# Attention scores as 64x64 tiles, keys and queries in one transfer, and another order of the first batch's transfers

## The chip, the core and the metric

The kernel runs on one core of a Trainium2 chip. The metric is the device time of one execution in microseconds (us), lower is better. TensorE (PE in the profile) multiplies; VectorE (DVE), ScalarE (ACT) and GpSimd (POOL) do the rest; SyncE (SP) computes nothing and issues transfers, as ACT and POOL also can. Each engine works through its own instructions in the order in which the program issued them.

## The reference, cut to what matters

```python
# q, k, v: 8 batches x 8 heads x 576 positions x 64, float32
scores = q @ k.T / 8
# heads 0-3: the last 32 positions; heads 4-7: every 4th of the last 128
attn = softmax(where(mask, scores, -1e9))
x = (attn @ v) -> (8, 576, 512)
u = x + real(fft(fft(x, axis=1), axis=2))
un = layernorm(u)
out = u + relu(un @ w_ch1) @ w_ch2        # 512 -> 2048 -> 512
```

## The kernel before

All work is written down as operations with an engine, a cost, a priority and the buffers that they read and write. `Plan.run` then plays a list scheduler: each engine takes, among the operations whose inputs are there, the one of lowest priority number, and the order found in this way is the program of that engine. So costs and priorities in the text change the order of instructions, not only what they say.

Attention. A pair is two heads of one batch, and each batch has four pairs (two of the plain window, two of the dilated one, whose positions the host has reordered so that its window also is a band). `attend_pair` requests the keys (two transfers of 64 partitions, into the two diagonal blocks of a tile `kb` whose other blocks stay zero), the queries (one transfer, tile `tq`) and the values (`vt`). It then calls `attend` twice (u = 0 and 1), which the text calls an attend: 64 of them in all, 8 in a batch. An attend has 8 or 10 blocks of 64 queries. For each block one float32 matmul contracts all 128 partitions (line 617: queries of both heads against keys of one head and zeros) into 64 partitions and 96 columns of one PSUM bank. Two banks (`sc`) take turns, so that one attend's scores can be written while the last one's are read. DVE adds the mask and takes the row maximum (L636), ACT takes the exponential (L642), PE transposes the probabilities (L656), ACT copies them out of PSUM (L658, L662), PE multiplies with the values (L669), and DVE normalises into `xt` and, for the last 64 positions, `xl` (L682, L687). The `xl` tag has one buffer, so the plain pairs' `xl` has to wait until the dilated pairs' has been stored.

Mix. `store` sends the result to DRAM scratch in the order that the transform wants (for the plain pairs of batch 0 straight into SBUF tiles). `fold` loads it back (L814, L823) and adds mirrored rows (L826, L828, L840, L842). `along_seq` (L877) and `along_channels` (L923) are the two Fourier transforms as matmuls. `normalise` makes the rows of the feed-forward input, `turned` (L771, L779) transposes them for batch 0.

Feed-forward. 6 of the 16 blocks of the hidden dimension are run in the first part, as a `fill` for each pair of token tiles: 72 matmuls up (L1053), 36 down (L1069). Their weights, float64 in DRAM, are prepared on the chip (L995 to L1015) through the same ring of four buffers (`ut`) that holds the feed-forward inputs; buffers of a ring are handed out strictly in the order of the text. The other ten blocks run at the end (L1334, L1432, L1399), when attention's memory is free.

PSUM banks are lent between tags. The first `NPT2` attends use a bank that later belongs to `mix`, and the first `NAV2` attends one that later belongs to `ff`:

```python
views["av2"] = [pt_av[1], zs[0]]
views["pt2"] = [pt_av[0], mixes[1]]
plan.behind.update({"av": ("av2",), "ff": ("av2",), "pt": ("pt2",), "mix": ("pt2",)})
```

`behind` means that the first buffer of a tag is handed out only when every buffer of the other tag is done. So the first `mix` matmul comes after 14 attends, and the first fill after 21.

Until `ff` is first used, PE runs filler matmuls on a tile of zeros (L542) when nothing else is ready; they have the lowest priority of all and no result.

Of the kernel before, what the change touches and what calls it, by code (L numbers as in the profile page):

```python
# [9 lines left out]
F32 = mybir.dt.float32  # L10
# [17 lines left out]
NKB = 2  # L28
NV = 3
NTQ = 2  # L30
# [10 lines left out]
NPT2, NAV2 = 14, 21  # L41
NGANG = 4
NU0, NU1 = 9, 9
NFD, NUD, NLW = 1, 0, 0
P_QK0, P_V0 = -8, -7
P_ST, P_FD, P_WD, P_ST0, P_FD0, P_SPAN0, P_SPAN1 = -9.92, -2.8, -14.79, -21.37, -25.12, 7.59, 23.92
P_QK, P_V, P_TR, P_MIX, P_SPAN, P_W, P_WF, P_FILL, P_FILLT = -7.53, -11.06, -5.0, 3.7, 13.0, 27.01, 3.96, 47.55, 3.61
P_MIX0, P_MIX1 = -24.21, 7.67
NSEQ, NCHN = 3, 7
# [5 lines left out]
WIN = 32  # L55
DIL = 4
# [107 lines left out]
def columns(x):  # L164

    return np.ascontiguousarray(by_pair(x).swapaxes(4, 5).reshape(B, 2, 2, P, S))
# [14 lines left out]
class Buf:  # L181


    def __init__(self, make=None, tag=None, ap=None):
        self.make, self.tag, self.ap = make, tag, ap
        self.writer, self.readers = {}, {}
        self.left = 0
        self.free_at = None
# [11 lines left out]
PSUM_TAGS = ("sc", "pt2", "av2", "pt", "av", "mix", "ff", "duo0", "duo1", "duo2")  # L200


class Plan:
# [21 lines left out]
    def add(self, eng, cost, fn, r=(), w=(), prio=0.0, nbytes=0, at=0.0):  # L225
# [15 lines left out]
        for items, writes in ((r, False), (w, True)):  # L241
            for it in items:
# [7 lines left out]
                else:  # L250
                    b.readers.setdefault(key, []).append(op.num)
        op.bufs = list(bufs.values())
# [8 lines left out]
    def run(self):  # L261
# [5 lines left out]
        dma = 0.0  # L267
# [36 lines left out]
        while events:  # L304
# [4 lines left out]
            while again:  # L309
                again = False  # L310
                for eng in busy:
# [48 lines left out]
                    if got.nbytes:  # L360
                        dma = max(dma, end + 0.9) + got.nbytes / (PIPE0 if end < T_PIPE else PIPE1)
                        done = dma + 1.6
                        lanes[eng].append(done)
                        heapq.heappush(events, done)
# [55 lines left out]
def fused_kernel(ctx: ExitStack, tc, q, k, v, w1, w2, seq, tail, chn, alt, mask, ident, perm, flip, out):  # L420
# [24 lines left out]
    views = {"sc": pair, "pt": pt_av[:1], "av": pt_av[1:], "mix": mixes, "ff": zs}  # L445
# [4 lines left out]
    plan.behind.update({"duo0": ("sc",), "duo1": ("pt", "av"), "duo2": ("mix",)})  # L450
# [27 lines left out]

    flip_sb = Buf(ap=const.tile([P, 16], I32, name="flip_sb")[:, 0:8])
# [25 lines left out]
    kbs = [fixed(heads, [P, 2, WIN + S], F32, f"kb{i}") for i in range(NKB)]  # L505
# [9 lines left out]
    def send(b, out_, in_, r, w, prio, nbytes):  # L515
        on, eng, cost = (nc.sync, "SP", 0.5) if b else (nc.gpsimd, "POOL", 0.55)
# [4 lines left out]
    def start():  # L521
# [9 lines left out]
        for n, t in enumerate(kbs):  # L531
            on, eng = (nc.gpsimd, "POOL") if n else (nc.vector, "DVE")
# [990 lines left out]
```

## Time and profile before

| | us |
|---|---|
| median of 3 runs | 1051.65 (1048.65 to 5732.28) |
| the profiled execution, its own time | 1049.0 |
| its span, first to last instruction | 1047.2 |
| PE busy, share of the span | 98% |
| mean granted TensorE clock | 0.991 |

The span is the part that the trace shows; 1.8 us lie around it. All rows below are of that one execution, with times counted from the start of the span. PE's busy time holds the filler matmuls and the pipeline's latency too, so 98% is not the share of useful work.

### The profile page before, as it was taken

What the parts mean: (1) busy time and instruction counts of PE and PEld (TensorE: products, weight loads), DVE (VectorE), ACT (ScalarE), POOL (GpSimd) and SP (SyncE); (2) the same over time, 40 slices, a digit from 0 to 9 for tenths busy, and PEclk for the clock granted to TensorE, in tenths of its full rate; (3) what the DMA queues carried; (4) which work ended last, traced back from release to release, by engine and by line L of the source; (5) the groups of instructions that cost most, each with busy time, mean ns of one, the idle gap of its engine ahead of it and who ended that gap; (6) DMA issues with size and microseconds to landing.
All of it is one profiled execution on the core that took longest, in us unless ns stands there. A gap on an engine that the chain in (4) does not pass through costs nothing.

```text
span 1047.2 us, 22363 instructions
## 1 busy us (share of the span) xinstructions
PE 1027.8 (98%) x8397; PEld 927.7 (89%) x8397; DVE 745.3 (71%) x2142; ACT 474.9 (45%) x1186; POOL 283.0 (27%) x339
## 2 busy tenths in 40 slices
PE   8899999999999999999999999999999999999998
PEld 7789888888888888998999899999999999999987
DVE  5687776777676866787777576767676767676846
ACT  4545674455544533434443443535352525252522
POOL 1634415364353633553321110101010101010200
PEclk9889999999999999999999999999999999999999
DMA  9984887576656526335364212332323232222221
GB/s 241 287 241 132 243 238 213 158 202 193 198 153 180 167 70 185 111 101 162 103 193 112 88 41 56 107 75 89 85 90 86 77 102 73 93 71 92 81 62 41
DMA packets 104903, 138.51 MB, mean 132 GB/s; under 512 B 10791, under 2 KB 64138, under 8 KB 104795
## 3 DMA queue, kind: packets, MB, share of 16 engines
q1 hardware_dynamic: 100554, 127.29, 43.2%
q0 software_dynamic: 3696, 8.97, 3.1%
q8 instruction: 66, 1.08, 0.4%
q10 hardware_dynamic: 544, 0.82, 0.2%
q14 instruction: 43, 0.34, 0.1%
HBM read 99.24 MB, written 37.21 MB: 130 GB/s over the span
## 4 chain that ended last, share of the span: by engine, by line
PE 73%; DVE 3%; DMA 3%; POOL 1%; issue 1%; SPq 0%; ACT 0%; DVEq 0%; POOLq 0%; ACTq 0%
PE bank L1334 23%; PE bank L1432 20%; PE bank L1069 11%; PE bank L1053 10%; PE bank L923 3%; PE bank L877 2%; DMA tq<-in_q_dram 1%; PE bank L1399 1%; PE bank L617 1%; PE bank L669 1%; PE bank L656 1%; DMA ut<-us 1%; DVE low L1061 0%; PE bank L899 0%; DVE ut L1176 0%
## 5 line engine op out<-in xcount | busy, mean ns | idle before, releaser
L1334 PE MATMUL bank<-low,wb 128*128 128x512 f32 x1080 | 255.6, 389 | 0.0
L1334 PEld LDWEIGHTS bank<-low,wb 128*128 128x128 f32 x1080 | 198.0, 188 | 36.9
L1053 PE MATMUL bank<-ut,low 128*128 128x256 f32 x1296 | 167.3, 282 | 0.2
L1053 PEld LDWEIGHTS bank<-ut,low 128*128 128x128 f32 x1296 | 157.1, 188 | 2.9 <-DVE low L1061 0.8
L1069 PE MATMUL bank<-low 128*128 128x512 f32 x648 | 153.1, 391 | 0.1
L1097 POOL DMA_INDIRECT ut<-us,flip_sb x20 | 39.8, 1990 | 396.8 <-DVE ut L1154 243.5
L1069 PEld LDWEIGHTS bank<-low 128*128 128x128 f32 x648 | 119.6, 188 | 24.4 <-DVE low L1061 0.3
L1340 ACT ACTIVATE xa<-bank 128x256 f32<-128x256 f32 x90 | 34.3, 381 | 171.0 <-PE bank L1334 171.0
L642 ACT ACTIVATE pm<-pm,mx 128x96 f32<-128x96 f32 x256 | 81.7, 369 | 54.6 <-DVE mx L636 53.5
L1371 DVE TENSOR_TENSOR y<-xa 128x384 f32<-128x384 f32 x45 | 25.1, 558 | 97.1 <-ACT xa L1340 95.1
L1176 DVE STREAM_TRANSPOSE ut<-ut 128x512 f32<-128x512 f32 (+1 forms) x76 | 71.0, 974 | 14.0 <-DMA ut<-us 12.8
L1143 DVE TENSOR_TENSOR ut<-ut,bank 128x512 f32<-128x512 f32 (+1 forms) x136 | 73.1, 547 | 2.2
L1432 PEld LDWEIGHTS bank<-w2s,low 128*128 128x128 f32 x588 | 71.7, 188 | 2.1
L1061 DVE SCALAR_TENSOR_TENSOR low<-bank,low 128x256 fp32r<-128x256 f32 x108 | 45.2, 420 | 39.3 <-ACT low L1059 38.5
L1432 PE MATMUL bank<-w2s,low 128*128 128x256 f32 x588 | 72.1, 278 | 0.0
L1059 ACT ACTIVATE low<-bank 128x256 fp32r<-128x256 f32 x108 | 41.2, 381 | 67.5 <-PE bank L1053 67.3
L636 DVE CUSTOM_DVE_ANT_0 pm<-bank,mask_sb 128x96 f32<-128x96 f32 x256 | 53.1, 249 | 13.5 <-PE bank L617 13.1
L617 PE MATMUL bank<-kb,tq 128*64 128x96 f32 x1152 | 58.4, 249 | 2.9 <-DMA tq<-in_q_dram 2.7
L1432 PEld LDWEIGHTS bank<-w2s,hm 128*128 128x128 f32 x483 | 58.9, 188 | 1.8
L1432 PE MATMUL bank<-w2s,hm 128*128 128x256 f32 x483 | 59.2, 278 | 0.0
L617 PEld LDWEIGHTS bank<-kb,tq 128*64 128x64 f32 x1152 | 50.3, 138 | 5.2 <-issue 4.0
L1013 ACT CAST low<-y 128x640 fp32r<-128x640 f32 (+1 forms) x50 | 35.8, 715 | 40.0 <-DVE y L1373 27.0
(174 smaller groups left out, 1836.6 us busy)
## 6 DMA issues: line engine op xcount, KB each, us to landing
vt<-in_v_dram SPq DMA_DIRECT2D x32, 438.8 KB
us<-uc SPq DMA_DIRECT2D x36, 257.0 KB
tq<-in_q_dram SPq DMA_DIRECT2D x32, 288.0 KB
part<-row SPq DMA_DIRECT2D x36, 256.0 KB
wst<-in_w_dram SPq DMA_DIRECT2D x18, 512.0 KB
ut<-us SPq DMA_DIRECT2D x36, 256.0 KB
ut<-part SPq DMA_DIRECT2D x36, 256.0 KB
kb<-in_k_dram SPq DMA_DIRECT2D x62, 144.0 KB
```

The source lines that it names most:

```text
L617: nc.tensor.matmul(sc()[QB * h:QB * h + QB, KB * i:KB * i + KB], lhsT=tq()[:, QB * t:QB * t + QB], rhs=kb()[:, e, QB * t:QB * t + KB], sta ...
L636: nc.vector.tensor_tensor_reduce(prob(i), sc()[:, KB * i:KB * i + KB], mask_sb()[:, kind], -0.125, 3.0e38, ALU.add, ALU.min, mx()[:, i:i + 1],
L642: add("ACT", 0.265, lambda i=i: nc.scalar.activation(out=prob(i), in_=prob(i), func=AF.Exp, bias=mx()[:, i:i + 1], scale=-1.0), ((mx, i),) ...
L1053: nc.tensor.matmul(z()[:, :n_tok], lhsT=wf()[a][:, kk], rhs=ut()[:, p, kk], start=(kk == 0 and n == 0), stop=(kk == KT - 1 and n == 2),)
L1059: add("ACT", act(n_tok) - 0.05, lambda: nc.scalar.activation(out=h()[:, 0, :n_tok], in_=z()[:, :n_tok], func=AF.Relu), (z,), ((h, 0),), prio)
L1061: add("DVE", dve(n_tok), lambda: nc.vector.scalar_tensor_tensor(h()[:, 1, :n_tok], z()[:, :n_tok], 0.0, h()[:, 0, :n_tok].bitcast(F32), op ...
L1069: nc.tensor.matmul(acc(), lhsT=h()[:, a, P * s:P * s + P], rhs=wf()[:, p], start=(first and n == 0), stop=(last and n == 2),)
L1097: add("POOL", 1.04, lambda: nc.gpsimd.indirect_dma_start(dst(), None, us[idx // 4](), bass.IndirectOffsetOnAxis(ap=flip_sb()[:, 4 * kk + i ...
L1143: add("DVE", dve(C if at in (outer, inner) else TOK1), lambda: nc.vector.tensor_tensor(out=blocks(part())[:, at], in0=blocks(part())[:, at ...
L1176: nc.vector.transpose(out=o[back], in_=x[:, g])
L1334: nc.tensor.matmul(z(), lhsT=wb1[NF1 + 2 * p + f]()[:, a, kk], rhs=ut()[:, x, kk], start=(kk == 0 and n == 0), stop=(kk == KT - 1 and n == 2),
L1432: nc.tensor.matmul(acc()[block // 2][:, TOK1 * (block % 2):TOK1 * (block % 2) + TOK1], lhsT=part(hl, a, i, i + 1), rhs=w2s[p]()[:, j, x], ...
```

## The change

- Scores (line 617 before): each block is now a 64x64 tile of the array. It contracts only its own head's 64 partitions, and the two heads write to two PSUM banks. Rows (head) and columns (which of two blocks) alternate, so four tiles of the array are named in turn. One `sc` buffer is now the pair of banks, so there is one instead of two. The mask step of the last block of an attend with u = 1 is two instructions (one per bank), 32 more in all.
- Scores of an attend are planned behind the PSUM copy of the attend two before it from the third attend on (`NGANG` 4 to 2).
- Keys and queries of a pair lie side by side in DRAM and come in one transfer of 128 partitions into `qk` (same bytes), three such tiles instead of two; the zero blocks and their clearing are gone. Batch 0's fourth pair borrows two buffers of the `ut` ring for its keys, queries, values, and the plain pairs' `xt` and `xl`, so all of batch 0 can be requested at the start.
- Batch 0's plain results go out from ACT and POOL in place of POOL and SP, and its fold loads are issued by POOL in place of SP. The clearing of a scratch row is released at 15 + 20 b in the plan.
- The tables of the transforms: the channel tables are requested after attend 0 (was 7), the sequence tables after attend 5 (was 3).
- Weight preparation: all six up blocks first, then the six down blocks (they alternated). The two feed-forward inputs of batch 0 take their place in the ring after 7 and 9 preparations (both after 9).
- `NPT2` 14 to 13, `NAV2` 21 to 16, new priorities, and a plan in which queues share the transfers' rate.

```diff
-NPT2, NAV2 = 14, 21
-NGANG = 4
-NU0, NU1 = 9, 9
+NPT2, NAV2 = 13, 16
+NGANG = 2
+NU0, NU1 = 7, 9
-P_MIX0, P_MIX1 = -24.21, 7.67
-NSEQ, NCHN = 3, 7
+P_MIX0, P_MIX1 = -2.89, 6.05
+NSEQ, NCHN = 5, 0
+Q_ST0, Q_X0, Q_PL0 = "PPPP", "P", "AP"
...
+    ta, tb = utb(), utb()
+    nv, nx = 2 * NB * (D + 1), 4 * P
+    lent = [within(ta, 0, GAP + 2 * S), within(tb, 0, nv, KB, "p (e t d) -> p e t d", e=2, d=D + 1),
+            within(tb, nv, nx, P, "p (m h d) -> p m h d", m=2, d=D), within(tb, nv + nx, P, P, "p (j d) -> p j d", j=2)]
...
-        for e in range(2):
-            ps = slice(64 * e, 64 * e + 64)
-            add(eng, 0.5, lambda e=e, ps=ps: on.dma_start(out=kb()[ps, e, WIN:], in_=k[b, dil, j, ps]),
-                (), ((kb, ("k", e)),), lead, 64 * S * 4)
-        dma(lambda: nc.sync.dma_start(out=tq(), in_=q[b, dil, j]), (), (tq,), lead, P * S * 4)
+        add(eng, 0.5, lambda: on.dma_start(out=qk_()[:, GAP:].rearrange("p (x s) -> p x s", x=2), in_=qk[b, dil, j]),
+            (), ((qk_, "qk"),), lead, 2 * P * S * 4)
...
+        def score(e, t, h, i):
+            rows = slice(QB * e, QB * e + QB)
+            nc.tensor.matmul(
+                sc()[e][QB * h:QB * h + QB, KB * i:KB * i + KB], lhsT=qk_()[rows, GAP + S + QB * t:GAP + S + QB * t + QB],
+                rhs=qk_()[rows, GAP - WIN + QB * t:GAP - WIN + QB * t + KB], start=True, stop=True,
+            )
+
         def scores():
-            for i, (lanes, _, _) in enumerate(slabs):
-                for h, (e, t) in enumerate(lanes):
-                    nc.tensor.matmul(
-                        sc()[QB * h:QB * h + QB, KB * i:KB * i + KB], lhsT=tq()[:, QB * t:QB * t + QB],
-                        rhs=kb()[:, e, QB * t:QB * t + KB], start=True, stop=True,
-                    )
+            for i in range(2):
+                for h in range(2):
+                    for e in range(2):
+                        score(e, 4 * u + 2 * i + h, h, i)
+            if u:
+                for e in range(2):
+                    score(e, NB - 1, e, 2)
...
         for i, (_, kind, _) in enumerate(slabs):
+            for e in ((i % 2,) if i < 4 else range(2)):
+                ps_ = slice(0, P) if i < 4 else slice(QB * e, QB * e + QB)
...
-            f, eng = n // 2, "DVE" if n < NLW else "POOL"
-            if n % 2 == 0:
+            f, x = (n % NF1, n // NF1) if PREPM else divmod(n, 2)
+            if x == 0:
```

## Rows read from the trace of the kernel before

**Rows 1.** The page: busy time, share of the span and instructions of each engine.
```profile
PE 1027.8 (98%) x8397; PEld 927.7 (89%) x8397; DVE 745.3 (71%) x2142; ACT 474.9 (45%) x1186; POOL 283.0 (27%) x339
```
**Rows 2.** Chain that ended last: start, duration, what it was.
```profile
578.86 19.04 PE bank L1334 x84
...
1029.03 13.91 PE bank L1399 x90
```
**Rows 3.** Longest of PE's waits, 0 to 580: total us, times, longest.
```profile
PE bank L656 <- ACT pm L642: 6.9, 6, 2.6
```
**Rows 4.** Stretches: length, busy us of PE, PEld, DVE, ACT, POOL, PEclk, DMA, GB/s.
```profile
0.00:40.00 40.00, 32.86 (x395) 29.63 (x397) 22.95 (x124) 19.47 (x54) 12.93 (x25) 0.87 1.03 260
...
0.00:117.00 117.00, 104.74 (x1275) 95.77 (x1275) 83.24 (x397) 62.42 (x175) 44.88 (x69) 0.93 0.87 236
...
117.00:380.00 263.00, 260.51 (x2844) 230.55 (x2844) 193.62 (x854) 140.55 (x409) 117.18 (x164) 1.00 0.64 182
...
579.00:1047.20 468.20, 463.92 (x2955) 420.36 (x2953) 321.03 (x603) 193.09 (x435) 41.21 (x23) 1.00 0.28 78
```
**Rows 5.** First 117 us by line (PE, PEld): filler L542, L617, L669, L656.
```profile
0.00:117.00 117.00, 49.64 (x290) 42.65 (x290) 0.93 0.87 236
...
0.00:117.00 117.00, 20.95 (x412) 18.32 (x412) 0.93 0.87 236
...
0.00:117.00 117.00, 16.82 (x376) 14.15 (x376) 0.93 0.87 236
...
0.00:117.00 117.00, 20.49 (x100) 11.86 (x100) 0.93 0.87 236
```
**Rows 6.** Groups by line (busy us, mean ns, idle before); then L617 after 117 us.
```profile
L617 PE MATMUL bank<-kb,tq 128*64 128x96 f32 x1152 | 58.4, 249 | 2.9 <-DMA tq<-in_q_dram 2.7
...
L669 PE MATMUL bank<-vt,ptsb 96*64 96x65 f32 x1152 | 48.8, 232 | 0.4 <-ACT ptsb L662 0.3
...
117.00:380.00 263.00, 37.45 (x740) 31.94 (x740) 1.00 0.64 182
```
**Rows 7.** Timeline of PE, one attend: start, us, operation, count.
```profile
169.38 0.80 PE L669 MATMUL bank<-vt,ptsb 96*64 96x65 f32 x20
170.02 1.00 PE L617 MATMUL bank<-kb,tq 128*64 128x96 f32 x20
170.94 0.64 PE L656 MATMUL bank<-ident_sb,pm 128*96 128x128 f32 x4
```
**Rows 8.** Timeline of all engines, 28 to 119 us, the steps to the first fill.
```profile
28.28 1.71 PE L617 MATMUL bank<-kb,tq 128*64 128x96 f32 x36
...
52.27 0.28 DVE L687 TENSOR_SCALAR xl<-bank,rinv 128x64 f32<-128x64 f32 x1 [0.97 <-DMA xsm<-xl]
...
53.41 1.27 PE L669 MATMUL bank<-vt,ptsb 96*64 96x65 f32 x36
...
66.49 0.42 DVE L826 TENSOR_TENSOR t<-x,x 128x257 f32<-128x257 f32 x1
...
71.80 0.58 ACT L658 COPY ptsb<-bank 96x512 f32<-96x512 f32 x1 [0.96 <-PE bank L669]
...
74.58 1.65 PE L877 MATMUL bank<-seq,ees 128*128 128x290 f32 x6
...
101.83 0.69 DVE L779 TENSOR_TENSOR ut<-bank,ut 128x512 fp32r<-128x512 f32 x1 [0.44 <-ACT ut L778]
...
115.23 0.42 DVE L682 TENSOR_TENSOR xt<-bank,rinv 128x256 f32<-128x256 f32 x1
...
118.91 1.66 PE L1053 MATMUL bank<-ut,low 128*128 128x256 f32 x12
```
**Rows 9.** Groups by line: the mask step on DVE (busy us, mean ns).
```profile
L636 DVE CUSTOM_DVE_ANT_0 pm<-bank,mask_sb 128x96 f32<-128x96 f32 x256 | 53.1, 249 | 13.5 <-PE bank L617 13.1
```
**Rows 10.** One weight block: its transfer's issue; its last step on POOL.
```profile
106.27 0.33 SPq L995 DMA_DIRECT2D ut<-in_w_dram  x1
...
L1015 POOL TENSOR_TENSOR low<-ut,low x1: 1273/1273/1273, 120.2 to 120.2; 128x512 fp32r<-128x512 f32 x1
```

More of the change, by code (lines that the diff above doesn't have):

```diff
@@ L251, in add @@
                     b.readers.setdefault(key, []).append(op.num)
+        for b in list(bufs.values()):
+            if b.parent is not None:
+                bufs[id(b.parent)] = b.parent
         op.bufs = list(bufs.values())
@@ L360, in run @@
                     if got.nbytes:
-                        dma = max(dma, end + 0.9) + got.nbytes / (PIPE0 if end < T_PIPE else PIPE1)
-                        done = dma + 1.6
+                        begin = max(pipe.get(eng, 0.0), end + 0.9)
+                        took = got.nbytes / (PIPE0 if end < T_PIPE else PIPE1)
+                        others = [x for x in pipe if x != eng and pipe[x] > begin]
+                        pipe[eng] = begin + took * (1 + len(others))
+                        for x in others:
+                            pipe[x] += took
+                        done = pipe[eng] + 1.6
                         lanes[eng].append(done)
@@ L477, in utb, with within, make @@
         return ffnb("ut", [P, 2, KT, TOK1], F32R, NUT)
+    def within(t, lo, n, rows=P, how=None, **sizes):
+        def make():
+            x = t().rearrange("p i k t -> p (i k t)")[:rows, lo:lo + n].bitcast(F32)
+            return x.rearrange(how, **sizes) if how else x
+        return Buf(make, parent=t)
+    ta, tb = utb(), utb()
+    nv, nx = 2 * NB * (D + 1), 4 * P
+    lent = [within(ta, 0, GAP + 2 * S), within(tb, 0, nv, KB, "p (e t d) -> p e t d", e=2, d=D + 1),
+            within(tb, nv, nx, P, "p (m h d) -> p m h d", m=2, d=D), within(tb, nv + nx, P, P, "p (j d) -> p j d", j=2)]
     flip_sb = Buf(ap=const.tile([P, 16], I32, name="flip_sb")[:, 0:8])
@@ L504, in fused_kernel @@
     gone = fixed(heads, [1, 1], F32, "gone")
-    kbs = [fixed(heads, [P, 2, WIN + S], F32, f"kb{i}") for i in range(NKB)]
+    qks = [fixed(heads, [P, GAP + 2 * S], F32, f"qk{i}") for i in range(NQK)]
     blank = fixed(heads, [P, 2 * P], F32R, "blank")
@@ L515, in send @@
     def send(b, out_, in_, r, w, prio, nbytes):
-        on, eng, cost = (nc.sync, "SP", 0.5) if b else (nc.gpsimd, "POOL", 0.55)
+        on, eng, cost = {"S": (nc.sync, "SP", 0.5), "P": (nc.gpsimd, "POOL", 0.55), "A": (nc.scalar, "ACT", 0.5)}[b]
         add(eng, cost, lambda: on.dma_start(out=out_(), in_=in_()), r, w, prio, nbytes)
@@ L584, in attention @@
         for n, dil in enumerate((0, 1) if b else (1, 0)):
-            xts = [attw("xt", [P, 2, 4, D], F32, NXT) for _ in range(2)] + [attw("xl", [P, 2, D], F32, 1)]
+            if b or not n:
+                xts = [attw("xt", [P, 2, 4, D], F32, NXT) for _ in range(2)] + [attw("xl", [P, 2, D], F32, 1)]
+            else:
+                xts = [attw("xt", [P, 2, 4, D], F32, NXT), lent[2], lent[3]]
             for j in range(2):
@@ L725, in store @@
             for n, (dst, src, o, i) in enumerate(put):
-                send(b, o, i, (src,), (((plus, minus)[dst], (dil, u, n)),), early, P * 2048 // len(put))
+                send("S" if b else Q_ST0[n % len(Q_ST0)], o, i, (src,), (((plus, minus)[dst], (dil, u, n)),), early, P * 2048 // len(put))
             return
@@ L1222, in fill @@
         for s, idx in enumerate(tiles):
-            acc = bank("sc" if late else "ff")
+            acc = bank("sc1" if late else "ff")
             for f in range(NF1):
```

85 lines of the change are left out of this document (42 added, 43 removed).

## The prediction

> **What bounds the kernel now.** I began with the page's busy shares: PE leads with 98%, DVE has 71% [rows 1]. The chain of waits ends in PE: from 579 us on it is the last ten hidden blocks back to back, untouched by the change, so what counts is when that stretch may begin [rows 2]. PE's own waits before it are short, 6.9 us for the longest kind [rows 3]. So PE bounds the kernel, but a busy PE is not a useful one, and the next view to read is stretches. After 117 us PE is busy 260.5 of 263 us with attention, mix and fills [rows 4], and work removed there is time removed, as fills wait in store behind it. Before 117 us it is busy 104.7 us, of which 49.6 us are the filler on zeros [rows 4, 5]. So 117 - 104.7 + 49.6 = 61.9 us of that stretch carry no useful work. DMA is the busy part there: a share of 1.03 at 260 GB/s over the first 40 us, 0.87 at 236 GB/s over the 117, against 0.64 later [rows 4]. The granted clock is below 1.00 on average there (0.87, 0.93), that is, partly the lower of its two levels [rows 4]; while PE has spare time, that costs nothing by itself.
>
> What ends the stretch? The timeline shows two gates, and both are the borrowed banks. The first mix matmul (74.58) comes 2 us after the copy at 71.80, the 14th of its kind, though its folded input began at 66.49; the first fill (118.91) comes 3.3 us after the DVE step at 115.23 that frees the 21st attend's bank, though its transposed input was there from 102.5 [rows 8]. The count fits NAV2: 376 value instructions at 18 to an attend are 20.9 attends [rows 5]. The change lowers the gates to 13 and 16.
>
> **Scores.** 576 blocks give 1152 matmul instructions, two to a float32 block [rows 6]. In a block of 20 the busy time less one instruction's 249 ns, over the other 19, is (1.00 - 0.249) / 19 = 39.5 ns; for values (0.80 - 0.232) / 19 = 29.9 ns [rows 6, 7]. Per moving column that is 0.41 (96) and 0.46 ns (65), so both go with the columns streamed and not with a fixed price of an instruction. No row shows four tiles of the array. Bounds: if four overlap where two do now, 39.5 / 2 = 19.8 ns; if the array gives no more overlap, 39.5. 29.9 is the quickest pair of weight load and multiply that the trace has. I take 25, midway between 19.8 and 29.9, since the block is streaming, but it comes near a pace that nothing here has yet beaten. On the path lie the 740 instructions after 117 us [rows 6]: 740 x 14.5 ns = 10.7 us (0 to 14.6). Those before it only make room for filler.
>
> The Trainium skill ("TensorE: Matmul & The Clock Gate", "Wait — 56ns, not 53.3ns?") says that matmuls never start closer than about 25 ns. By it the upper end would be 10.7 us in place of 14.6; the value blocks at 29.9 ns don't contradict it, and no row tests it.
>
> Where the array changes its form there is a gap. From the start of this block of 20 to the whole-array transposes are 0.92 us, of which 20 x 39.5 ns are streaming: 0.13 us are left; from values to scores 0.64 - 20 x 29.9 ns = 0.04 us [rows 7]. Values and scores have the same width in columns now, and the trace mostly shows them next to each other; afterwards scores have 64 rows and values 96. So each attend can have one more change, at 0.04 to 0.13 us: 740 / 18 = 41 attends after 117 us give 1.6 to 5.3 us. I take 0.09, midway, as these neighbours differ in one dimension only: 3.7 us. Scores net: 10.7 - 3.7 = 7.0 us.
>
> The Trainium skill ("TensorEngine Tiling (Array Packing)", "Key Properties") says that a change of tiling mode, not of tile, drains TensorE. This speaks against the change; the 0.13 us agree, and by it the upper end, 5.3 us, would be the one to take, and scores net 5.4 us.
>
> **Single buffer for scores.** The next attend's scores now wait until DVE has read the last pair of banks. A mask step takes 53.1 / 256 = 0.21 us [rows 9], so DVE needs about 0.9 us. Behind a waiting score stand all later PE instructions. I cost it at nothing: 41 attends in 263 us are one per 6.4 us, and fills, mix and values lie between. Without that cover it is up to 0.9 us an attend (a rival, below). The 32 extra masks are 32 x 0.21 = 6.7 us of DVE, two thirds of it where DVE is busy 194 of 263 us [rows 4]: no bound.
>
> **The first stretch.** Batch 0's last attend had its scores at 28.28, but its values only at 53.41: the plain pairs' `xl` waited until 52.27 for the dilated pairs' to be stored [rows 8]. The borrowed `xl` takes this wait away. Batch 0's inputs are 4 x 1.04 MB from the shapes, with masks and permutations 4.9 MB, or 19 us at 260 GB/s, plus landing. So I estimate its last scores at 24 to 28 and its values at 30. (Its first transfer is as large as the three it replaces; the clearings were hidden.) From the whole stretch an attend takes 115 / 21 = 5.5 us, so the 13th is done at 30 + 5 x 5.5 = 57 and the 16th at 74. Mix took from 74.58 to 102.5, 28 us, to the first fill's input; from 57 that is 85. With the 3.3 us from gate to matmul the first fill starts at 88. Transfers allow that: two batches' inputs 8.3, constants and tables 3.5, seven weight blocks 3.7, stores and loads of x 3.6, the next pair 1.0, together 20 MB, are 85 us at 236 GB/s. So 118.9 - 88 = 31 us earlier. But 5 of 21 attends then come after the gate. One costs PE 0.92 + 0.64 us for scores and values of 20 instructions and some 0.5 us of transposes (0.64 for four less a latency) [rows 7], 1.9 us over both sizes, 1.64 with cheaper scores: 5 x 1.64 = 8.2 us come back. Early net: 31 - 8 = 23 us.
>
> Bounds: if mix can't begin before its fold of 66 us, and only the gate of 21 goes, the fill starts at 102.5 + 3.3 = 106, and 13 - 8 = 5 us are left. If attends go at the pace that transfers of 1.04 MB a pair allow at 260 GB/s (2 us each), mix begins at 42 and the fill at 73; weights and tables must share, so I allow 80: 39 - 8 = 31 us. Below nothing: fold loads now stand on POOL's queue behind 1.6 MB of sequence tables (6 us at 260 GB/s), and two borrowed buffers leave two for weights until batch 0 is through. If both put mix back by 10 us against the trace, the fill starts after 129, a loss of 10 us.
>
> **Weights.** The ring gives out no buffer past the first fill's input until that exists, so five down blocks come after it where two down and one up block did. From the transfer's issue (106.27) to the last step's end (121.5) are 15 us [rows 10]; two buffers turn, so three rounds, 45 us, in place of two. From 6 us before the fill starts they end 39 us after it. PE has in that time 72 + 24 up matmuls (the twelve at 118.91 take 1.66 us with one latency, so 0.12 each [rows 8]: 11 us), 8 attends (13 us) and the next mix (about 10 us): 34 us. 5 us of shortage: I take them off. None if rounds take 13 us, 15 if the next mix is late.
>
> **ACT's issues.** Five of batch 0's plain stores now stand in ACT's queue; each waits for DVE, and exponentials stand behind it. Some 0.5 us each, in the first stretch, beside filler; without that cover 2.5 us.
>
> **Sum.** 7 + 23 - 5 = 25 us: 1049.0 - 25 = 1024 us for the profiled execution's time; the median shown lies 2.7 us above that, and I keep to the profiled one, rounding to 1025.
>
> **Rivals.**
> 1. *The early gain doesn't come* (fill at 106 or the weights take all): 7 + 5 - 5, 1042 us. For it: the fold waits on transfers, and DMA is full. Against: the gates explain both starts to 2 and 3 us.
> 2. *Four tiles overlap no more than two.* The two instructions of a float32 block stand next to each other on one tile, so in order the second waits for the first, and only the neighbour tile overlaps: 39.5 ns stays and changes cost 3.7 us: 23 - 5 - 4, 1035 us. For it: 0.41 and 0.46 ns a column.
> 3. *Both go well*: fill at 80, 19.8 ns, no shortage: 14.6 - 2 + 31, 1005 us at its best, 1012 likely.
> 4. *Slower: the one score buffer binds.* Where a planned order puts DVE's other work ahead of the masks, PE stands for 0.9 us an attend on all 41, and the 5 moved: 41 us against 25 of gain, 1065 us. It decides from 0.55 us an attend on. Against it: DVE is free a quarter of the time. Together with the fill at 129 it is the only way up that I see.
>
> **How the numbers follow.** Chances: forecast 0.45 (1017 to 1034), rival 1 0.18, rival 2 0.12, rival 3 0.17, rival 4 0.08. A measurement of this kernel can tell about 2% from no change, 21 us: the bound lies at 1028. The forecast's cases below it are 0.33 of 0.45, with rival 3 and a little of rival 2 0.53; slower 0.06; the rest 0.41. The range, 1005 to 1045, leaves out rival 4 and the far ends of 1 and 3.
>
> **What would show it.** Scores: their group's busy time near 58.4 x 25 / 39.5 = 37 us; near 58 rival 2. Values and scores: start-to-start a tenth of a us longer. Gates: first mix matmul near 57, first fill near 88, filler under 30 us. Weights: PE's idle or wait on the down blocks' last step after the first fill. Rival 4: PE waiting at the scores for the mask line. I am wrong if the fill starts after 106 or the scores' block of 20 takes over 0.85 us.

## The result, and the profile after

The changed kernel takes 1022.04 us (median of 4 runs, 1020.46 to 1022.74) against 1050.96 for the kernel before, a ratio of 0.973 with a 95% interval of 0.9707 to 0.9752. Its profiled execution took 1022.3 us with a span of 1020.5, so the two profiled executions differ by 26.7 us, where the sum had 25. One of the four executions of the kernel before took 5732.28 us; the ratio is over the other three.

The page, first part, answers to [rows 1]; the chain of waits (start, duration, what it was), around the start of its last stretch, to [rows 2]:

```profile
PE 1006.4 (99%) x8347; PEld 898.2 (88%) x8347; DVE 750.4 (74%) x2203; ACT 479.4 (47%) x1186; POOL 291.4 (29%) x348
```

```profile
545.14 6.80 PE bank L1096 x30
551.94 16.32 PE bank L1361 x72
```

PE is as busy as before by its share; the page alone shows no reason for the gain. The chain shows where it lies: the last ten hidden blocks start at 551.94 instead of 578.86 and take as long as before (468.6 us to the end of the span, 468.3 before). So everything happened ahead of them. Stretches of the changed kernel (columns as in [rows 4]; the last of the four was 171.66 us busy before):

```profile
0.00:40.00 40.00, 36.50 (x517) 32.13 (x521) 22.60 (x151) 21.77 (x62) 15.33 (x36) 1.00 1.00 307
0.00:117.00 117.00, 111.18 (x1481) 96.40 (x1483) 95.00 (x474) 74.50 (x211) 54.59 (x85) 1.00 0.91 274
117.00:380.00 263.00, 260.11 (x2796) 226.78 (x2796) 196.73 (x860) 139.53 (x391) 113.53 (x157) 1.00 0.57 172
380.00:552.00 172.00, 170.77 (x1122) 154.73 (x1121) 126.11 (x255) 70.17 (x150) 69.30 (x76) 1.00 0.46 135
```

Groups by line (busy us, mean ns of one, idle before): filler, scores, their mask step, in answer to [rows 5, 6, 9]. The row of the scores lacks the 36 matmuls of the pair with the borrowed buffer, which have another tile name and take 1.4 us: all 1152 take 41.7 us, 58.4 before.

```profile
L558 PE MATMUL bank<-blank 128*128 128x256 f32 x240 | 40.3, 311 | 1.2 <-DVE blank L553 1.2
L632 PE MATMUL bank<-qk 64*64 64x96 f32 x1116 | 40.3, 254 | 0.9 <-DVE mx L663 0.9
L663 DVE CUSTOM_DVE_ANT_0 pm<-bank,mask_sb 128x96 f32<-128x96 f32 x256 | 55.5, 247 | 11.6 <-PE bank L632 10.4
```

Read together these give the account. PE's busy time without filler, up to the last stretch, was 104.74 - 49.64 + 260.51 + 198.66 = 514.3 us [rows 4, 5; the last term is the stretch 380 to 579], and is 111.18 - 40.3 + 260.11 + 170.77 = 501.8 us. So of 26.9 us, 12.5 are work that PE no longer has, and the other 14.4 are idle time and filler (64.6 us before, 50.2 now). In the first 117 us the useful work rises from 55.1 to 70.9 us. The granted clock there is 1.00 (0.93 before), so part of the 12.5 us is the same work at the higher of the two levels. The kernel before ran 17.1 us at the lower level, in three stretches that begin at 15.4, 32.5 and 70.0 us, and PE was busy 9.1 us of them with work other than filler. If that work took twice its time, 4.5 us of the 12.5 are the clock; this is an estimate from those rows.

The timeline, steps that answer to [rows 8]:

```profile
36.90 0.80 PE L696 MATMUL bank<-ut,ptsb 96*64 96x65 f32 x20
...
55.74 0.42 DVE L875 TENSOR_TENSOR ees<-ee,ees 128x257 fp32r<-128x257 f32 x1
...
56.16 0.99 PE L904 MATMUL bank<-seq,ees 128*128 128x290 f32 x6
...
76.81 0.41 DVE L709 TENSOR_TENSOR xt<-bank,rinv 128x256 f32<-128x256 f32 x1
...
86.04 0.68 DVE L806 TENSOR_TENSOR ut<-bank,ut 128x512 fp32r<-128x512 f32 x1
86.44 0.71 PE L1080 MATMUL bank<-ut,low 128*128 128x256 f32 x3
...
105.72 0.50 PE L1096 MATMUL bank<-low 128*128 128x512 f32 x1
```

Batch 0's last values come at 36.90 (53.41 before), the first mix matmul at 56.16 (74.58), the first fill at 86.44 (118.91). Neither gate holds any more. The copy of the 13th attend ends at 51.7, 4.5 us before the first mix matmul, whose folded input is done only at 56.16 (L875). The 16th attend frees its bank at 77.2, 9 us before the fill; what releases the fill now is its input: its first two matmuls read only the part that was ready, the third waits for L806, done at 86.72. The first product down comes at 105.72.

### The profile page after: what moved, and what is told of

The parts are those of the page before. It is cut to its first block, busy times and chain, and to the rows that moved or that the text cites. A ratio compares the mean times of both kernels' runs of the same rounds, so it can differ in the third digit from the quotient of the medians.

```text
span 1020.5 us, 22187 instructions
## 1 busy us (share of the span) xinstructions
PE 1006.4 (99%) x8347; PEld 898.2 (88%) x8347; DVE 750.4 (74%) x2203; ACT 479.4 (47%) x1186; POOL 291.4 (29%) x348
## 4 chain that ended last, share of the span: by engine, by line
PE 84%; DVE 8%; DMA 4%; issue 1%; ACT 1%; POOL 1%; ACTq 0%; SPq 0%; DVEq 0%; POOLq 0%
PE bank L1361 24%; PE bank L1459 20%; PE bank L1096 12%; PE bank L1080 11%; PE bank L950 3%; PE bank L696 3%; PE bank L683 3%; PE bank L632 2%; PE bank L558 2%; PE bank L904 2%; DMA ut<-in_w_dram 2%; PE bank L1426 1%; DVE pm L663 1%; DVE low L1088 1%; DMA ut<-us 1%
## 5 line engine op out<-in xcount | busy, mean ns | idle before, releaser
L1096 PE MATMUL bank<-low 128*128 128x512 f32 x648 | 155.8, 393 | 0.0
L669 ACT ACTIVATE pm<-pm,mx 128x96 f32<-128x96 f32 x256 | 83.7, 370 | 55.5 <-DVE mx L663 52.3
L663 DVE CUSTOM_DVE_ANT_0 pm<-bank,mask_sb 128x96 f32<-128x96 f32 x256 | 55.5, 247 | 11.6 <-PE bank L632 10.4
L1116 ACT COPY row<-bank 128x512 f32<-128x512 f32 x36 | 21.0, 585 | 66.2 <-PE bank L1096 59.2
L1459 PE MATMUL bank<-low 128*128 128x256 f32 x420 | 51.5, 278 | 0.0
```

Source lines behind the costliest of these rows:

```text
L663: nc.vector.tensor_tensor_reduce(prob(i)[ps_], sc()[e][ps_, KB * (i // 2):KB * (i // 2) + KB], mask_sb()[ps_, kind], -0.125, 3.0e38, ALU.a ...
L669: add("ACT", 0.265, lambda i=i: nc.scalar.activation(out=prob(i), in_=prob(i), func=AF.Exp, bias=mx()[:, i:i + 1], scale=-1.0), ((mx, i),) ...
L1096: nc.tensor.matmul(acc(), lhsT=h()[:, a, P * s:P * s + P], rhs=wf()[:, p], start=(first and n == 0), stop=(last and n == 2),)
L1459: nc.tensor.matmul(acc()[block // 2][:, TOK1 * (block % 2):TOK1 * (block % 2) + TOK1], lhsT=part(hl, a, i, i + 1), rhs=w2s[p]()[:, j, x], ...
```

## How the four tiles share the array

The group's mean of 254 ns hides the pace, and so does one number for a block. Windows of 50 or 60 ns, each set in the next round, count the matmuls under way, of the line with the scores alone. Each is under way for some 245 ns, so these counts are sums of what has started. First the kernel before (the burst of 20 at 170.02), then the changed one (at 159.94); columns: stretch, length, PE busy (count), clock, DMA share, GB/s.

```profile
170.02:170.08 0.06, 0.06 (x2) 1.00 0.84 307
170.11:170.16 0.05, 0.05 (x4) 1.00 0.77 287
170.19:170.24 0.05, 0.05 (x6) 1.00 1.00 369
```

```profile
159.94:160.00 0.06, 0.06 (x4) 1.00 0.49 171
160.08:160.14 0.06, 0.06 (x8) 1.00 0.01 0
160.16:160.21 0.05, 0.05 (x12) 1.00 0.00 0
```

Two matmuls start together in each round before, four after: the four tiles run beside each other. In the trace the 20 starts of this burst lie at 0, 7, 13, 20; 133, 140, 147, 153; 216 to 236 and 298 to 318 (four each); 381, 401; 463, 483 ns. So a round lasts 82 ns, the first one 133 (in the kernel before also 82, the first 87), and a burst of 16 is four rounds of four. The first four records are 50 ns longer than the others (293 against 243 ns), so the ends of the rounds are 82 ns apart from the first on. The other four of a burst of 20 belong to the last two query blocks, which stand on two tiles only, (0,0) and (1,1): two more rounds of two. A burst of 16 and one of 20 in the timeline:

```profile
105.23 0.56 PE L632 MATMUL bank<-qk 64*64 64x96 f32 x16
...
109.38 0.73 PE L632 MATMUL bank<-qk 64*64 64x96 f32 x20
```

From these durations it is (0.56 - 0.254) / 15 = 20.4 ns for the first 16, and (0.73 - 0.56) / 4 = 42.5 ns for the last four. Over all 19 steps it is (0.73 - 0.254) / 19 = 25.1 ns.

The Trainium skill ("TensorEngine Tiling (Array Packing)", "Key Properties") says that tiles work independently of each other, and the four starts within 60 ns agree. The floor of 25 ns between starts which the prediction cited from it ("TensorE: Matmul & The Clock Gate", "Wait — 56ns, not 53.3ns?") does not hold between tiles here: the measurement decides. The kernel before had already broken it, with starts at 0 and 7, 87 and 93 ns; the prediction looked only at means over a block.

## The experiments

Each ratio is against the kernel before, run on the same chip. "Changed" in the table is the time above.

| run | us | ratio, 95% interval |
|---|---|---|
| changed | 1022.04 | 0.9730 (0.9707 to 0.9752) |
| e1 scores alone, on the kernel before | 1043.75 | 0.9938 (0.9919 to 0.9957) |
| e5 gates alone, on the kernel before | 1053.90 | 1.0039 (1.0017 to 1.0061) |
| e2 128 rows | 1031.34 | 0.9824 (0.9805 to 0.9843) |
| e3 one head after the other | 1021.97 | 0.9733 (0.9707 to 0.9760) |
| e13 one tile after the other | 1024.26 | 0.9745 (0.9717 to 0.9774) |
| e14 128 columns | 1025.58 | 0.9767 (0.9742 to 0.9791) |
| e4 gates back | 1036.77 | 0.9871 (0.9843 to 0.9899) |
| e6 `xl` shared | 1042.87 | 0.9934 (0.9916 to 0.9952) |
| e11 nothing lent | 1029.12 | 0.9798 (0.9772 to 0.9824) |
| e12 three transfers | 1040.64 | 0.9925 (0.9891 to 0.9959) |
| e15 two transfers | 1028.02 | 0.9793 (0.9768 to 0.9819) |
| e8 weights back | 1032.11 | 0.9831 (0.9797 to 0.9865) |

All but e1 and e5 start from the changed kernel. In e2, e3, e13 and e14 the programs of the other engines are the changed kernel's own; in the others the scheduler made a new order for all engines, with priorities that stayed those of the kernel from which the run starts. A difference from the changed kernel compares runs that were not made together; beside them the kernel before had medians of 1049.94 to 1050.96 us. The intervals reach some 2 to 4 us to either side, so the times of the changed kernel, e3, e13 and e14 hardly differ, and there the bursts decide.

**e1, the scores alone.**

```diff
-                        sc()[QB * h:QB * h + QB, KB * i:KB * i + KB], lhsT=tq()[:, QB * t:QB * t + QB],
-                        rhs=kb()[:, e, QB * t:QB * t + KB], start=True, stop=True,
+                    sc()[e][QB * h:QB * h + QB, KB * i:KB * i + KB], lhsT=tq()[rows, QB * t:QB * t + QB],
+                    rhs=kb()[rows, e, QB * t:QB * t + KB], start=True, stop=True,
...
+    views = {"sc": [lambda: pair], "sc1": pair, "pt": pt_av[:1], "av": pt_av[1:], "mix": mixes, "ff": zs}
```

> The kernel before with only the 64x64 score tiles (one pair of banks, the split mask of the last block, the lower planned cost). My term for scores: 25 ns an instruction in place of 39.5 after the first fill, less a longer gap at each attend, 7 us net: 1042 us. The borrowed banks still hold the first fill to 21 attends, so it stays between 110 and 120 us. Rival (the scores carry most of the whole gain, since cheaper attends also pull the start): 1030 us or less, first fill before 100. Rival (the single score buffer costs what the tiles give): 1049 us.

Measured: 1043.75 us, 6.8 less than the kernel before on that chip (1050.54). The rows of its filler and its scores:

```profile
L542 PE MATMUL bank<-blank 128*128 128x256 f32 x390 | 60.0, 301 | 1.2 <-DVE blank L537 1.2
L617 PE MATMUL bank<-kb,tq 64*64 64x96 f32 x1152 | 43.5, 256 | 4.4 <-DMA tq<-in_q_dram 3.2 <-DVE mx L646 1.0
```

The scores' busy time falls by 14.9 us, the filler rises by 10.4: what attention saves ahead of the first fill turns into filler, since nothing else may run there. After 117 us the scores fall from 37.45 to 27.77 us, 9.7 us where the prediction had 10.7 before the change of form. So the term of 7 us agrees with 6.8, but not all of the 6.8 need be the tiles: e1's four executions had a granted clock of 0.996 to 1.000, the seven of the kernel before 0.990 to 0.997, and the one at 0.997 took 1047.65 us, 3.9 more than e1.

**e2, full rows** keeps the two banks and contracts 128 partitions again. Each score is then the sum of both heads' scores, so the output is not the reference's.

```diff
-lhsT=qk_()[rows, GAP + S + QB * t:GAP + S + QB * t + QB],
-rhs=qk_()[rows, GAP - WIN + QB * t:GAP - WIN + QB * t + KB], start=True, stop=True,
+lhsT=qk_()[:, GAP + S + QB * t:GAP + S + QB * t + QB],
+rhs=qk_()[:, GAP - WIN + QB * t:GAP - WIN + QB * t + KB], start=True, stop=True,
```

> The changed kernel, each score matmul contracting all 128 partitions again (so it adds up both heads' scores: the output is not the reference's); same plan, same order of instructions. If tiles in different rows overlap, the block of 20 goes back from 0.73 to about 1.00 us and the time rises by 7 to 10 us, to 1030, less what the missing change of form between values and scores gives back (up to 0.1 us an attend). Rival (the new pace is that of an instruction, not of overlapping): block of 20 stays 0.73 us, time 1022.

Measured: 1031.34 us; timeline, a burst of 20 and one of 16:

```profile
163.14 1.05 PE L632 MATMUL bank<-qk 128*64 128x96 f32 x20
...
172.74 0.93 PE L632 MATMUL bank<-qk 128*64 128x96 f32 x16
```

A burst of 20 is back at 1.05 us, (1.05 - 0.25) / 19 = 42 ns: with two tiles the old pace returns. So the 64 rows carry the pace, not the two banks, and in this order they are worth 9.3 us.

**e3 and e13, other orders within a burst.** e3 takes all blocks of one head before those of the other; e13 also keeps consecutive blocks on one tile.

```diff
-            for i in range(2):
-                for h in range(2):
-                    for e in range(2):
+            for e in range(2):
+                for i in range(2):        # e13: h, then i
+                    for h in range(2):
```

> The changed kernel with the four blocks of one head before those of the other, so that neighbours differ in the columns of the array only, as before the change; form and contraction stay at 64 rows. Overlap theory: pace within a head about 39.5 ns, block of 20 near 0.95 us, time 1028. Rival (64 rows are quicker by themselves): block of 20 stays at 0.73 us, time 1022.

> The changed kernel with the score matmuls reordered so that consecutive blocks of a burst stay on one 64x64 tile of the array before the next tile is used (work and numbers the same). In the changed kernel a block of 20 is 0.73 us busy, a pace of (0.73 - 0.254)/19 = 25 ns, and e3, which kept the blocks of two tiles alternating, left that as it was. Theory A, that the pace needs matmuls of at least two tiles running beside each other: the pace falls back to the 40 ns of the 128x64 tiles of the kernel before or worse, block of 20 at 1.0 us or more, and the time about as in e2, 1030 us or more. Theory B, that a matmul which contracts 64 rows is issued every 25 ns whatever its neighbour is: block of 20 stays at 0.73 and the time at 1022, plus or minus 3.

Measured: 1021.97 and 1024.26 us; a burst of 20 is 0.74 and 0.75 us. The same count of matmuls under way in e13 (burst at 159.86):

```profile
159.86:159.91 0.05, 0.05 (x4) 1.00 0.48 164
159.99:160.06 0.07, 0.07 (x8) 1.00 0.02 0
160.08:160.13 0.05, 0.05 (x12) 1.00 0.00 0
```

The pace hardly depends on the order. It would be hasty to read this as "64 rows are quick by themselves", as the expectations did: the counts are the same four to a round, even where the text names one tile for two blocks in turn. Both theories had assumed that PE stands still when the next matmul's tile is busy. The rows speak against that. Two windows from the start of a burst in e3 (at 108.75), then in e13 (at 109.28), count the first round: of the four, two and four have started by 20 and 40 ns in e3, two and three in e13.

```profile
108.75:108.77 0.02, 0.02 (x2) 1.00 0.66 205
108.75:108.79 0.04, 0.04 (x4) 1.00 0.57 180
```

```profile
109.28:109.30 0.02, 0.01 (x2) 1.00 0.60 205
109.28:109.32 0.04, 0.04 (x3) 1.00 0.62 205
```

In the trace they lie at 0, 7, 13, 20 ns in the changed kernel, at 0, 7, 27, 33 in e3 and at 0, 13, 27, 40 in e13, in 61 of the 64 bursts of each. In the program, the first matmul instructions on the four tiles have 0, 2, 4, 6 others before them in the burst, 0, 2, 8, 10 in e3 and 0, 4, 8, 12 in e13 (two instructions to a block): 3.3 ns for each in all three. So the starts of a round are one on each tile, and a matmul whose tile is busy doesn't hold up those behind it on other tiles, at least within a burst. That TensorE starts its instructions in the order of the program, as is said of every engine at the outset, does not hold here. Another order moves only the offset of the last tile (20, 33, 40 ns), and with it the 0.73, 0.74 and 0.75 us.

**e14, 128 columns instead of 96.**

```diff
-sc()[e][QB * h:QB * h + QB, KB * i:KB * i + KB], ...
-rhs=qk_()[rows, GAP - WIN + QB * t:GAP - WIN + QB * t + KB], ...
+sc()[e][QB * h:QB * h + QB, KB * i:KB * i + P], ...
+rhs=qk_()[rows, GAP - WIN + QB * t:GAP - WIN + QB * t + P], ...
```

> The changed kernel with each score matmul moving 128 columns in place of 96; the 32 added columns belong to the next block and are overwritten by it, so the scores that are used are the same. Theory A, that the pace of 25 ns is the streaming of the columns: 25 x 128/96 = 33 ns, block of 20 at 0.254 + 19 x 0.033 = 0.89 us, which over 64 pairs with four bursts of some 18 blocks is about 64 x 72/4 x 0.008 = 9 us of TensorE, and the time 1026 to 1031. Theory B, that it is a price for each instruction: block of 20 stays at 0.73 to 0.76, time 1022, plus or minus 3.

Measured: 1025.58 us; timeline:

```profile
161.91 0.89 PE L632 MATMUL bank<-qk 64*64 64x128 f32 x20
...
171.40 0.67 PE L632 MATMUL bank<-qk 64*64 64x128 f32 x16
```

The burst takes the 0.89 us of theory A. With its mean of 280 ns a burst of 16 gives (0.67 - 0.280) / 15 = 26.0 ns, 1.27 times the 20.4 for 1.33 times the columns, and a round goes from 82 to 109 ns, 1.32 times: streaming, with room for a fixed price of a few ns at most. The time, 3.5 us more, lies just under theory A's 1026 to 1031, but only 1.3 us above e13 on the same chip; it is the burst that decides.

**e4 and e5, the gates.** e4 puts them back in the changed kernel, e5 moves them in the kernel before and does nothing else.

```diff
-NPT2, NAV2 = 13, 16
+NPT2, NAV2 = 14, 21        # e4; e5 the other way round
```

> The changed kernel with the gates of before, 14 and 21 attends. My gate theory: the first fill waits for the 21st attend (about 95 us at this kernel's pace), 9 us later than 86, and the time rises by some 9 less 5 attends' work of 8, that is 1 to 5 us: 1023 to 1027. Rival (the mix chain sets the first fill here, not the gate of 16): the first fill moves only as far as the 21st attend lies after the mix chain's end. Rival (gates are the whole early gain): 1040 us.

> The kernel before with only the two gates lowered to 13 and 16 attends. My theory: batch 0's last values still wait until about 53 for the shared xl, so mix may start a few us before 74.6 (fold at 66.5 is its floor), and the first fill at 102 to 106 in place of 118.9: 13 us earlier less 5 attends of 1.9 us: 1043 to 1046 us. Rival (gates are most of the early gain): 1035 us or less, first fill before 95. Rival (the gates of before were not binding, only near): 1050 us.

Measured: e4 1036.77, 14.7 us more than the changed kernel; e5 1053.90, 4.0 us more than the kernel before on that chip (1049.94). Both missed their expectations. In e5 the first fill does come at 105.17, 13.7 us earlier, as reckoned. Stretch 117 to 200 of e5 and, in the second fence, of the kernel before:

```profile
117.00:200.00 83.00, 77.40 (x918) 65.81 (x917) 59.85 (x293) 48.32 (x145) 34.50 (x44) 0.98 0.79 214
```

```profile
117.00:200.00 83.00, 82.00 (x962) 71.16 (x962) 60.54 (x287) 48.68 (x144) 31.53 (x42) 1.00 0.75 205
```

PE is idle 5.6 us there instead of 1.0: filler ends with the first fill, and the first product down comes hardly earlier (153.22, against 154.93). The products down of a fill come after all 72 of its matmuls up, and the sixth up block, the eleventh of the twelve in the old order, is done only at 149.25:

```profile
147.96 1.29 POOL L1015 TENSOR_TENSOR low<-ut,low 128x512 fp32r<-128x512 f32 x1 [4.14 <-ACT low L1013]
```

```profile
149.75 1.31 PE L1053 MATMUL bank<-ut,low 128*128 128x256 f32 x9
...
153.22 0.85 PE L1069 MATMUL bank<-low 128*128 128x512 f32 x3
```

Moved alone, the gate turns filler into idle time. In the changed kernel, where the sixth up block is done at 91.92, putting the gates back costs 14.7 us. The first fill then starts at 97.28, close to the 95 that was expected, so the step that failed is the price: filler is 45.8 us instead of 40.3, idle time ahead of the last stretch 14.9 instead of 9.9, and the rest is work that takes longer. One stretch of e4:

```profile
120.00:160.00 40.00, 36.59 (x427) 28.59 (x424) 30.87 (x153) 23.69 (x66) 20.18 (x23) 0.87 0.62 191
```

The changed kernel has 38.89 us busy and a clock of 1.00 there. In e4 PE waits 2.5 us in all between 141 and 149, mostly for attention's copies and masks, and from 148.4 to 158.7 the granted clock is at its lower level. PE is busy 9.2 us of that, so the clock costs up to 4.6 of the 14.7 us (an estimate).

**e8, the weights' order back.**

```diff
-NU0, NU1 = 7, 9
+NU0, NU1 = 9, 9
-PREPM = 1
+PREPM = 0
```

> The changed kernel with the weights' preparation put back into its old order and place (no part of it ahead of the others, the old split over the engines' slots). My prediction charged the new order of the weights with 5 us of shortage. Theory A, that the charge is real: the time falls to about 1017 us. Theory B, that the new order is what feeds the first up and down products in time: first up after 88 us, first down after 108 us, and the time 1025 or more. If neither, 1022 plus or minus 3.

Measured: 1032.11 us, 10.1 more. Last step of a weight block on POOL (count, min/median/max ns, first and last start), changed kernel and e8:

```profile
L1042 POOL TENSOR_TENSOR low<-ut,low x12: 1272/1285/1387, 31.7 to 135.1; 128x512 fp32r<-128x512 f32 x12
```

```profile
L1042 POOL TENSOR_TENSOR low<-ut,low x12: 1278/1289/1760, 31.1 to 146.2; 128x512 fp32r<-128x512 f32 x12
```

The last block is ready 11 us later, the first fill starts at 90.85 (86.44), the first product down at 133.16 (105.72). It is again the sixth up block that sets the product down: it is done at 130.74 in e8 and at 91.92 in the changed kernel. Theory B holds: the new order, with the earlier place of the first fill's input, is a gain, where the prediction took off 5 us.

**e6 and e11, the borrowed buffers.** e6 gives the plain pairs of batch 0 the shared `xl` again; e11 borrows nothing, so all four buffers of the ring go to weights and inputs from the start.

```diff
-                xts = [attw("xt", [P, 2, 4, D], F32, NXT), lent[2], lent[3]]
+                xts = [attw("xt", [P, 2, 4, D], F32, NXT), lent[2], attw("xl", [P, 2, D], F32, 1)]     # e6
...
-    ta, tb = utb(), utb()
+    ta = tb = None                                                                                      # e11
```

> The changed kernel, with batch 0's plain pairs writing their last rows to the one shared xl buffer again instead of the borrowed one. My theory, that this wait held batch 0: its last attend's values come after 45 us in place of 37, first mix matmul some 8 us later than 56, time 1028 us. Rival (the wait was an effect of the slow store queue of before and is gone with it): 1022 us, mix at 56.

> The changed kernel with nothing borrowed from the ring of ut buffers: batch 0's fourth pair takes the next regular buffers for keys, queries, values and xt and the shared xl, so its inputs are requested when the first pair's are free, and all four ut buffers serve the weights at once. My theory: first mix matmul 8 to 12 us later, time 1030. Rival (three buffers of each kind were enough, and two more weight buffers help): 1022 us or a little less.

Measured: e6 1042.87 (20.8 more), e11 1029.12 (7.1 more). e11's time is as expected, though its first mix matmul is only 4.8 us later (60.99), not 8 to 12. e6 is a miss. Its first mix matmul is 4 us later (60.34), its first fill 4 us; yet PE loses time long after that. Two of its stretches, then the same of the changed kernel:

```profile
160.00:200.00 40.00, 37.16 (x389) 32.25 (x388) 30.03 (x131) 20.34 (x58) 14.30 (x20) 0.91 0.58 165
420.00:460.00 40.00, 36.03 (x229) 32.86 (x229) 28.60 (x63) 13.61 (x30) 27.91 (x32) 0.96 0.44 131
```

```profile
160.00:200.00 40.00, 38.96 (x409) 34.21 (x408) 30.88 (x127) 19.00 (x52) 20.14 (x29) 1.00 0.57 169
420.00:460.00 40.00, 39.70 (x276) 36.72 (x275) 30.08 (x66) 17.16 (x38) 21.93 (x24) 1.00 0.46 140
```

Batch 0's attention is over long before 440 us. This points to the new order that the scheduler makes, and not to the wait for `xl` itself, for most of the 20.8 us. The wait at 440 us is such a case:

```profile
441.51 0.67 ACT L1023 ACTIVATE wst<-wst 128x512 f32<-128x512 f32 x1 [7.25 <-DMA wst<-in_w_dram]
...
442.09 0.57 ACT L1116 COPY row<-bank 128x512 f32<-128x512 f32 x1
...
442.71 1.54 PE L1080 MATMUL bank<-ut,low 128*128 128x256 f32 x9 [3.56 <-ACT row L1116]
```

The copy that frees PE's bank stands on ACT behind a step of weight preparation that waits 7.25 us for its transfer. The granted clock is at its lower level from 167.1 to 174.0 and, right after this wait, from 443.6 to 447.0 (the 0.91 and 0.96 above): at most 5.1 us of the 20.8, by the same estimate. The other waits were not traced one by one. That e11, which gives up `xl` and more, loses only 7.1 fits this reading.

**e12 and e15, the merged transfer.** e12 splits it into the old three (keys in two halves, queries on SP); e15 into two of 128 partitions, on the queue of the merged one.

```diff
-        add(eng, 0.5, lambda: on.dma_start(out=qk_()[:, GAP:].rearrange("p (x s) -> p x s", x=2), in_=qk[b, dil, j]),
-            (), ((qk_, "qk"),), lead, 2 * P * S * 4)
+        for x in range(2):                                                                              # e15
+            add(eng, 0.5, lambda x=x: on.dma_start(out=qk_()[:, GAP + S * x:GAP + S * x + S], in_=qk[b, dil, j, :, x]),
+                (), ((qk_, ("qk", x)),), lead, P * S * 4)
```

> The changed kernel with each pair's keys and queries again in three transfers (two of 64 partitions, one of 128), into the same tile, no zero blocks. I cost the merge at nothing: 1022 us, first 40 us at about 300 GB/s. Rival (the one transfer is why the first 40 us move 307 GB/s in place of 260, and SP's three issues a pair hold up the others): 260 to 280 GB/s there, first mix matmul later than 60, time 1027 us or more.

> The changed kernel with the keys and the queries of a pair in two transfers of 128 partitions on the same queue, so that a partition's run in memory is 2304 bytes instead of 4608; order of queues as in the changed kernel. It tells apart two readings of e12 (1040.6 us, 260 GB/s in the first 40 us). Theory A, that the long rows make the early rate: 260 to 285 GB/s in the first 40 us in place of 307, first mix matmul at 60 us or later, and the time 1028 or more. Theory B, that e12 lost its time because the queries of the first pair stood behind others on SP and because of the 64-partition pieces: 295 GB/s or more, first mix matmul at 56 to 58 us, 1022 to 1026 us.

Measured: e12 1040.64 (18.6 more), e15 1028.02 (6.0 more). Stretches 0 to 40 and 40 to 80, of e12, e15 and the changed kernel:

```profile
0.00:40.00 40.00, 29.68 (x363) 26.72 (x364) 15.79 (x102) 14.95 (x41) 11.29 (x27) 0.87 0.97 260
40.00:80.00 40.00, 37.84 (x536) 32.97 (x535) 33.88 (x168) 27.16 (x78) 14.77 (x25) 1.00 0.90 259
```

```profile
0.00:40.00 40.00, 37.18 (x512) 33.08 (x513) 22.14 (x148) 20.20 (x57) 14.20 (x35) 1.00 1.02 303
40.00:80.00 40.00, 37.92 (x490) 33.62 (x489) 36.11 (x143) 25.39 (x72) 17.86 (x24) 0.96 0.79 226
```

```profile
40.00:80.00 40.00, 38.81 (x550) 34.05 (x543) 36.20 (x168) 28.16 (x80) 18.58 (x25) 1.00 0.88 263
```

In e12 the first pair's queries are issued on SP at 3.22, behind masks, permutations and values, and its first scores start at 11.23 (7.77 in the changed kernel):

```profile
3.22 0.43 SPq L619 DMA_DIRECT2D qk<-in_qk_dram  x1
...
11.23 0.56 PE L635 MATMUL bank<-qk 64*64 64x96 f32 x16 [1.88 <-DMA qk<-in_qk_dram]
```

The 260 GB/s of the first 40 us looked like the price of the short rows. e15 has rows as short (2304 bytes to a partition), and in the first 40 us 303 GB/s against 307: theory B holds for the rate. So the short rows don't explain e12's first 40 us. The place of the queries on SP, the pieces of 64 partitions and the new plan remain, all brought in by my edit, and they were not told apart. But e15's 1028 is theory A's time. Its rate is lower only from 40 to 80 us (226 against 263), its first fill comes at 88.94, its first product down at 110.21. So the merge is worth 6 us in this order; whether through the transfer or through the plan that goes with it is open.

## Why the prediction was right, and which terms were not

The forecast of 1025, in a range of 1005 to 1045, met 1022.04, and the signs of both halves of its sum (7 us from scores, 18 from the early stretch) are right. Step by step:

- *Scores, 7.0 us net*: e1 gives 6.8. Their busy time, forecast near 37 us, is 41.7. The pace of 25 ns is the mean that was measured, but not for the reason given. It isn't a value between two bounds: the bound of four overlapping tiles (19.8) is reached for 16 of 20 (20.4 ns), and the last four stay at the old 42.5. The prediction didn't look at which tiles the odd block falls on. Rival 2 is out: the second matmul of a block does wait a round, as it said, but the other three tiles fill it (the offsets in e3 and e13). That 25 is right as a mean is partly luck: a burst of 16 has 20.4.
- *The change of form, 0.09 us*: from the start of 20 value matmuls to the start of the scores it is now 0.73 us (108.65 to 109.38), 0.64 before.
- *One score buffer, at nothing*: PE waited at the scores for the mask step 0.9 us in the whole run. Rival 4 is out.
- *First stretch*: first mix matmul 57, measured 56.16; first fill 88, measured 86.44. The times are right, the reasons are not: the prediction got 57 from the 13th attend, and what the mix came right after is its folded input. Batch 0's last values are 7 us later than the 30 of the estimate, the next five attends quicker than its 5.5 us each, and the gate of 13 was open at 51.7. Nor does the gate of 16 hold the fill: its input does, as the prediction's chain from the mix has it.
- *8 us that come back through attends behind the gate*: too much. Before the first fill PE does 340 value instructions, 18.9 attends, where it did 396, 22.0: 3.1 attends come after it, 5 us at the prediction's price, and not five. By its own figures the 16th attend ends at 74 and the fill starts at 88, so attends fall between. By 117 us the changed kernel is ahead, with 448 value instructions (24.9 attends) against 376, and transfers at 274 GB/s against 236.
- *Filler under 30 us*: wrong, 40.3. The filler can't fall by what the fill is earlier, since e1's lesson holds here too: cheaper scores ahead of the fill become filler.
- *Weights, 5 us of shortage*: the wrong sign. The last block was done 50 us after the first fill (136.4), not 39, so the blocks came slower than reckoned; and still PE was busy 47.72 of the 49.96 us from 86.44 to 136.40. The step that failed is the 34 us of work that it gave PE for that time: it left out products down of finished blocks (from 105.72 on) and counted 8 attends where 10 were done. And it put all 5 us on the new order, without asking what the old one would do with the same early fill: that costs 10.1 us (e8).
- *The merged transfer, at nothing*: mis-sized by up to 6 us (e15).
- *The lower clock, at nothing*: doubtful. Of the 19 executions of the kernel before on e5's chip, the three with a mean granted clock of 0.996 or more took 1045.06 to 1045.78 us, the sixteen below it 1047.17 to 1053.5. Whether the clock makes these 5 us, or whatever idles PE early makes both, no run separates.
- *ACT's issues, at nothing*: not tried.

The errors in the early terms cancelled: of the 8 us for attends 3 were taken off and not lost, of the 5 for the weights all, and the 31 us of an earlier fill were too much. The fill came 32.5 us earlier, but filler and idle time up to the last stretch fell by 14.4. And the terms are not a sum: undone one at a time, gates, weights, loan, transfer and 64 rows cost 14.7, 10.1, 7.1, 6.0 and 9.3 us, 47 us together where the whole change gave 29, while the gates alone lose 4. Each delays the same last stretch, and each edit but that of the 64 rows gets a new order too. The order of the tables' requests, the queues of the stores and loads, the order of scores behind copies (`NGANG`) and the new priorities were never undone alone, so how the some 22 us beside the scores divide among all these is not shown.

## What to carry to other kernels

Where a chain of gates and inputs ends a stretch of filler, price the pieces together: a gate that opens before the weights are there turns filler into idle time (e5), and the same gate costs 15 us to put back once they are (e4). For small matmuls in a tiled array, count the rounds of the fullest tile, not the matmuls; in a plan made by a scheduler, an edit's cost holds only together with the order that it triggers, so look for idle time far from the edit before blaming it.

## What the runs showed of the hardware

- At a granted clock of 1.00, float32 matmuls on four 64x64 tiles start together, four in 20 ns, and each tile takes its next one 82 to 83 ns later for 96 columns (109 for 128, in e14): 0.85 ns a column and tile, and the same with two tiles of 128x64.
- A matmul whose tile was busy didn't hold up later ones on other tiles: a tile's first start came 3.3 ns later for each matmul that stood before it in the burst (changed kernel, e3, e13). The order in which the text names the tiles changed a burst of 20 by no more than 0.02 us (0.73, 0.74 and 0.75).
- Rows of 2304 or 4608 bytes to a partition made little difference to the rate of the first 40 us (303 and 307 GB/s).
